# More places for raw weight chunks, W' for two pages in a turn, and casts and exponentials one step later

## The chip, the cores and the metric

One core of a Trainium2 chip. The metric is the device time of one execution in microseconds; of the kernel before, three runs are shown, and one more execution was profiled. The engines run at the same time, each its own instructions in order: TensorE (PE, with weight loads as PEld), VectorE (DVE), ScalarE (ACT), GpSimd (POOL), and SyncE (SP), which here issues nearly all transfers.

## What is computed

An attention with 32 memory slots per head is followed by two layers of a feed-forward network, all in float32. Cut to what matters (4 batches, 8 heads, 576 tokens of 64 values each, 32 slots, 512 model values, 2048 hidden values):

```python
a = softmax(phi, over the 32 slots)            # with + 1e-9 in the divisor
k_m, v_m = einsum(a, k), einsum(a, v)          # per head, over the tokens
attn = softmax(q @ k_m.T / 8, over the slots)
x = (attn @ v_m), heads side by side           # (2304, 512)
h = maximum(x @ w_in, 0); x = h * h @ w_out    # first layer
h = x @ w_in2; out = h * tanh(softplus(h)) @ w_out2   # second layer
```

## The kernel before

**Tiling.** The attention output is never formed. For each batch the kernel makes W' = v_m times w_in (lines 484 to 511), so that h = softmax weights times W'. W' has 8 pages of 256 hidden values; a page serves two steps. Matrix products are made of three matmuls on a value split into a rounded high part and the rest (low part): ScalarE copies the high part, VectorE subtracts to get the low one.

**A tile** (`a_tile`, line 576) is a loop over steps fc, one for each 128 hidden values. A step has 6 matmuls of h = W' times the attention weights (lines 589 to 591), then ScalarE's Relu (597) and square (598), the split into g (602, 605), and, three steps later, 12 matmuls of g with w_out1 into four banks (551 to 553): 18 matmuls. The two halves (288 tokens each) of batches 0 and 1 are done in three groups of 4, 6 and 6 steps, 12 tiles in all (i = 0 to 11, line 729), so that each weight serves four tiles while it is converted. Batches 2 and 3 then take each half in one tile of 16 steps.

**Beside the steps** run: the conversion of the first layer's weights (`Conv`, line 149); the second layer's (`Fold`, line 236), whose results are stored by POOL (312); the memory k_m, v_m of the next batches (`kv_unit`); and the attention weights (`attn_unit`, line 443): score matmuls into a pair of banks, then transpose, maximum, difference (462), exponential (463), sum, product, transpose, and the split into ah and al (478, 479), cut into four parts by `yield`. A `lane` runs one part (or two) in each step. `tick` runs before the Relu of a step, `mid` and `post` after it.

**Conversion.** The weights come as 8-byte numbers, in 32 raw chunks of 512 KB, in the order of `order` (line 615). Count them from 0: chunk 20 is page row i1_10, 21 is i1_11, 22 is o1_10. A step starts one: ScalarE works on the high word (187), VectorE builds the float from bit fields (209, 216), and chunks of w_out are split (182, 224). Pages of w_in are also stored to DRAM (220), to be loaded again for batches 2 and 3 (`load_page`, 723). Nine chunks are loaded ahead; behind the bit fields of chunk n comes the load of chunk n+9 (222). Each load needs a place (`spots`, 623): chunks 0 to 17 have three places of the tag raw and six that later hold w_out1 (tags wo..7, wo..6, wo..5), in turn. From chunk 18 on there are the three raw places alone.

**W'.** `w_part` makes one page: 16 small matmuls into the bank pair "bb" (one buffer, also used by the score matmuls and by the transposes of phi), ScalarE's copy (495) and VectorE's subtraction (496). `w_pair` makes two pages in the two halves of the bank pair, and is used for batch 3 alone.

**Order.** The program is written in the order above, but a scheduler with a timeline of its own places each engine's instructions; earlier written work has the higher priority, and other work is drawn forward when it is ready. `issue_after` (in `behind`, 141) keeps an instruction behind a named one on the same engine. `marks["step"]` is the latest Relu.

Of the kernel before, what the change touches and what calls it, by code (L numbers as in the profile page):

```python
# [38 lines left out]
def body(tc, q, kvm, kvt, phi, w_in1, w_out1, w_in2, w_out2, out):  # L39
# [19 lines left out]
    cm_y, Y = open_pool("y", "right")  # L59
# [78 lines left out]
    marks = {}  # L138

    @contextlib.contextmanager  # L140
    def behind(table, key):

        if key is None:
            yield
        else:
            with tc.issue_after(table[key].ins):
                yield
# [295 lines left out]
    def attn_unit(b, half, nxt=None):  # L443
        n = f"{b}{half}"
        qt = q_t.pop((b, half))
        ps = banks2(f"psc{n}")
        for g in range(4):
            for p in range(2):
                done_pe["psc", b, half] = nc.tensor.matmul(
                    ps[M * g:M * g + M, p, :T], kT[b][D * p:D * p + D, M * g:M * g + M],  # L450
                    qt[g // 2][D * p:D * p + D, g % 2, :], start=True, stop=True)
        if nxt is not None:
            nxt()

        x = Y.tile([P, 2, T], F32, tag="x", name=f"x{n}", bufs=1)
        xv = x.rearrange("p a (c m) -> p (a c) m", m=NB)
        for p in range(2):
            nc.vector.transpose(x[:, p], ps[:, p, :T])
        mx = Y.tile([P, 2 * TB], F32, tag="smx", name=f"smx{n}", bufs=1)
        marks[b, half] = nc.vector.tensor_reduce(out=mx, in_=xv, op=ALU.max, axis=AX.X)  # L460
        yield
        nc.vector.tensor_sub(xv, xv, mx.unsqueeze(2).to_broadcast([P, 2 * TB, NB]))
        nc.scalar.activation(x, x, AF.Exp)
        yield
        sm = Y.tile([P, 2 * TB], F32, tag="ssm", name=f"ssm{n}", bufs=1)
        nc.vector.tensor_reduce(out=sm, in_=xv, op=ALU.add, axis=AX.X)
        nc.vector.tensor_scalar_add(sm, sm, EPS)
        nc.vector.reciprocal(sm, sm)
        nc.vector.tensor_mul(xv, xv, sm.unsqueeze(2).to_broadcast([P, 2 * TB, NB]))
        yield  # L470
        a = Y.tile([P, 2, T], F32, tag="at", name=f"at{n}", bufs=1)
        nc.vector.transpose(a.rearrange("p a t -> p (a t)"), x.rearrange("p a t -> p (a t)"))
        pool = Y if b in (1, 2) else X
        a_t[b, half] = tuple(
            pool.tile([P, 2, T], F32R, tag=f"a{part}", name=f"a{part}{b}{half}", bufs=2)
            for part in "hl")
        hi, lo = a_t[b, half]
        nc.scalar.copy(hi, a)
        marks[b, half] = nc.vector.tensor_sub(lo, a, hi.bitcast(F32))  # L479
        yield  # L480
# [3 lines left out]
    def w_part(b, j, lo, hi):  # L484

        ps = banks2(f"pw{b}{j}{lo}")[:, :, :hi - lo]
        for g in range(4):
            for p in range(2):
                nc.tensor.matmul(  # L489
                    ps[M * g:M * g + M, p], vT[b][D * p:D * p + D, M * g:M * g + M],  # L490
                    wt["i1", j][D * p:D * p + D, g, lo:hi], start=True, stop=True)
        if (b, j) not in wp:
            wp[b, j] = page([P, 2, 2, 256], F32R, f"wp{b}{j}")
        t = wp[b, j]
        nc.scalar.copy(t[:, 0, :, lo:hi], ps)
        nc.vector.tensor_sub(t[:, 1, :, lo:hi], ps, t[:, 0, :, lo:hi].bitcast(F32))  # L496

    def w_pair(b, j):

        ps = banks2(f"pw{b}{j}p")  # L500
        for i in range(2):
            for g in range(4):
                for p in range(2):
                    nc.tensor.matmul(
                        ps[M * g:M * g + M, p, 256 * i:256 * i + 256],
                        vT[b][D * p:D * p + D, M * g:M * g + M],
                        wt["i1", j + i][D * p:D * p + D, g], start=True, stop=True)
        for i in range(2):
            t = wp[b, j + i] = page([P, 2, 2, 256], F32R, f"wp{b}{j + i}")
            nc.scalar.copy(t[:, 0], ps[:, :, 256 * i:256 * i + 256])  # L510
            nc.vector.tensor_sub(t[:, 1], ps[:, :, 256 * i:256 * i + 256], t[:, 0].bitcast(F32))


    y1 = dram.tile([P, 4, NTOK], F32, name="y1")
# [61 lines left out]
    def a_tile(b, half, f0, f1, tick, mid, post, banks=("mm",)):  # L576

        acc = [psum.tile([P, 512], F32, tag=f"acc{d}", name=f"a{b}{half}{f0}{d}") for d in range(4)]
        done = evac_y1(b, half, f0 == 0, f1 == NF)
        hi, lo = a_t[b, half]  # L580
        for fc in range(f0, f1):
            n = f"{b}{half}_{fc}"
            w = wp[b, fc // 2]
            fs = slice((fc % 2) * P, (fc % 2) * P + P)
            ph = hbank(banks[fc % len(banks)], f"h{n}")[:, :T]
            key = ahead.get((b, half, fc))
            for hg in range(2):
                with behind(done_pe, key if hg == 0 else None):
                    nc.tensor.matmul(ph, w[:, 0, hg, fs], hi[:, hg], start=(hg == 0), stop=False)  # L589
                nc.tensor.matmul(ph, w[:, 0, hg, fs], lo[:, hg], start=False, stop=False)  # L590
                nc.tensor.matmul(ph, w[:, 1, hg, fs], hi[:, hg], start=False, stop=(hg == 1))  # L591
            tick(fc)
            flush()
            s = X.tile([P, T], F32, tag="s", name=f"s{n}", bufs=3)
            g = X.tile([P, 2, T], F32R, tag="g", name=f"g{n}", bufs=4)
            sh, sl = g[:, 0], g[:, 1]
            marks["step"] = nc.scalar.activation(s, ph, AF.Relu)  # L597
            nc.scalar.activation(s, s, AF.Square)

            def rest(s=s, sh=sh, sl=sl):  # L600
                if b < 3:
                    nc.scalar.copy(sh, s)  # L602
                else:
                    nc.vector.tensor_copy(sh, s)
                marks["lo"] = nc.vector.tensor_sub(sl, s, sh.bitcast(F32))  # L605

            later.append(rest)
            mid(fc)
            pend.append((mm2_step, (acc, fc, fc == f0, fc == f1 - 1, sh, sl, done)))
            run_pend(LAG)  # L610
            post(fc)


    bounds = [sum(GROUPS[:i]) for i in range(len(GROUPS) + 1)]
    order = []
    for f0, f1 in zip(bounds, bounds[1:]):
        order += [("i1", f0), ("i1", f0 + 1)]
        for f in range(f0, f1, 2):
            order.append(("o1", f))
            if f + 2 < f1:  # L620
                order += [("i1", f + 2), ("i1", f + 3)]
            order.append(("o1", f + 1))
    spots = [(Y, "raw", 3)] * 3 + [
        (wo, f"wo{part}{j}", 1) for j in (7, 6, 5) for part in "hl"]

    c1 = Conv(order, lambda i: spots[i % 9 if i < 18 else i % 3],
              lambda key, u: key != "i1" or u < 8 or (1, u // 2 - 4) in wp)
    c1.limit = 2 * GROUPS[0]
    c1.load(1)
# [37 lines left out]
    def lazy(f):  # L667
        yield from f()
# [19 lines left out]
    def attn_later(b, half):  # L688
        def nxt():
            if b < 2:  # L690
                if (b, half) == (0, 1):
                    load_q(1, 1)
                elif (b, half) == (1, 0):
                    load_q(2, 0)
                return
            nb, nh = (b, 1) if half == 0 else (b + 1, 0)
            if nb < B:
                load_q(nb, nh)
        return [[lazy(lambda: attn_unit(b, half, nxt)), 4]]


    subs = [(f0, f1, b, half) for f0, f1 in zip(bounds, bounds[1:])
# [20 lines left out]
    def load_page(j):  # L723

        wt["i1", j] = Y.tile([P, 4, 256], F32, tag="i1", name=f"win1r_{j}", bufs=4)
        nc.sync.dma_start(wt["i1", j], w1[j])

    lanes, n_steps = [], 1
    for i, (f0, f1, b, half) in enumerate(subs):
        final = i == len(subs) - 1  # L730
# [37 lines left out]
            run_step(lanes, n_steps)  # L768

        def post(fc):  # L770
            if fc % 2 == half == 0 and fc + 2 < f1 and i != 2:
                c1.need("i1", fc + 3)
                w_part(b, fc // 2 + 1, 0, 256)
            if i == 1 and fc + 1 == f1:
                w_part(1, fc // 2, 0, 256)
            if i % 4 == 0:
                if fc >= f0 + 2:
                    c1.need("o1", fc - 2)
                if fc + 1 == f1:
                    c1.need("o1", fc)  # L780
            if half == 1 and fc + 2 == f1 and not final:

                if b == 0:
                    w_part(1, f0 // 2, 0, 256)
                else:
                    c1.need("i1", f1 + 1)
                    w_part(0, f1 // 2, 0, 256)
            if final and fc < f1 - 1:
                w_part(2, fc - f0, 0, 256)
                if fc < f1 - 2:  # L790
                    load_page(fc - f0 + 2)

        if i == 0:
            w_part(0, 0, P, 2 * P)
# [17 lines left out]
            run_step(lane)  # L812

    def post(fc):
        if fc in (0, 2, 4):
            load_page(5 + fc // 2)
        if fc in (3, 5, 7):
            w_part(b, 5 + fc // 2 - 1, 0, 256)
        if fc == NF - 1:
            for j in range(4):  # L820
                load_page(j)
# [13 lines left out]
    drain(*lanes)  # L835


    while fold.busy():
        fold.tick()
    close(cm_psum2)  # L840
# [125 lines left out]
    now = 0  # L966
# [216 lines left out]
```

## Time and profile before

| | us |
|---|---|
| median of 3 runs | 766.96 (763.28 to 769.29) |
| the profiled execution | 767.97 |
| its span, first to last instruction | 766.1 |
| TensorE busy | 731.6 |
| VectorE busy | 530.1 |
| ScalarE busy | 424.8 |
| mean granted TensorE clock | 0.981 |

The busy time is a share of a span that has stages of different kinds: conversion and attention of batches 0 and 1 until about 200 us, batch 2 from 222.9, batch 3 from 318.2, and the second layer from 389.9 us on. PEclk is the clock that TensorE was granted, as a share of 2.4 GHz. A wait is put down to the instruction that released it. "Idle before" counts the time in which that engine did nothing before the instruction. Matmuls overlap, so the time from one start to the next tells more than the duration.

### The profile page before, as it was taken

To read this page: it belongs to the slowest core of one execution; us is meant where nothing else is said; L and a number is where in the kernel's file an instruction comes from. 1 tells how busy PE (TensorE), PEld (TensorE's weight loads), DVE (VectorE), ACT (ScalarE), POOL (GpSimd) and SP (SyncE) were. 2 spreads that over 40 slices of the span, in tenths; PEclk is the share of its full clock that TensorE was granted. 3 is DMA by queue.
4 is the path that set the end of the run, shared out by engine and by line. 5 is a ranking of instruction groups with operands and counts; after the bars stand their busy time and mean duration, and the time that the engine had idled before them with its cause. 6 is when DMAs were issued, how large, how long until landed. Compare 5 with 4: busy or idle time off the path is not lost.

```text
span 766.1 us, 15325 instructions
## 1 busy us (share of the span) xinstructions
PE 731.6 (95%) x5480; PEld 691.6 (90%) x5480; DVE 530.1 (69%) x1072; ACT 424.8 (55%) x960; POOL 130.9 (17%) x176
## 2 busy tenths in 40 slices
PE   5699799999999999999999999999999999999997
PEld 4487798998887889999999899989999989999997
DVE  3989835527587679787897856894756794556583
ACT  3677845756566678767665435652434652334552
POOL 0000000000121223323322401140411050111040
PEclk8699999999999999999999999999999999999999
DMA  8993505406898878787969989888977888787882
GB/s 330 404 409 108 174 20 195 136 1 214 309 324 280 305 242 314 275 313 238 364 211 324 343 250 364 250 256 276 339 244 264 252 256 290 235 267 240 263 271 73
DMA packets 87900, 195.80 MB, mean 256 GB/s; under 512 B 9872, under 2 KB 21136, under 8 KB 87824
## 3 DMA queue, kind: packets, MB, share of 16 engines
q1 hardware_dynamic: 78864, 165.45, 64.7%
q0 software_dynamic: 8960, 29.37, 9.7%
q8 instruction: 44, 0.72, 0.4%
q14 instruction: 32, 0.26, 0.1%
HBM read 151.78 MB, written 42.99 MB: 254 GB/s over the span
## 4 chain that ended last, share of the span: by engine, by line
PE 78%; DVE 7%; DMA 5%; ACT 5%; issue 3%; SPq 0%; POOL 0%; DVEq 0%; POOLq 0%; ACTq 0%
PE hb L995 7%; PE a L551 7%; PE hb L996 7%; PE hb L997 7%; PE a L553 7%; PE a L552 7%; PE h L589 4%; PE h L590 3%; PE h L591 3%; DMA raw_i<-in_moe_w_in_dram 2%; PE pw L489 1%; DVE opl L1040 1%; DMA yr<-y 1%; DMA raw_o<-in_moe_w_out_dram 1%; PE pk L407 1%
## 5 line engine op out<-in xcount | busy, mean ns | idle before, releaser
L551 PE MATMUL a<-g,o1h 128*128 128x288 f32 x512 | 150.2, 302 | 3.3 <-ACT g L602 3.3
L552 PE MATMUL a<-g,o1l 128*128 128x288 f32 x512 | 148.4, 298 | 0.0
L553 PE MATMUL a<-g,o1h 128*128 128x288 f32 x512 | 131.1, 298 | 0.4 <-DVE g L605 0.4
L1040 DVE TENSOR_TENSOR opl<-a,oph 128x384 fp32r<-128x384 f32 x144 | 92.9, 664 | 44.9 <-ACT oph L1039 44.3
L995 PE MATMUL hb<-ych,u 128*128 128x384 f32 x336 | 113.3, 337 | 2.7 <-DVE hs L1005 1.4
L996 PE MATMUL hb<-ycl,u 128*128 128x384 f32 x336 | 113.0, 336 | 0.0
L997 PE MATMUL hb<-ych,u 128*128 128x384 f32 x336 | 110.2, 336 | 0.0
L1039 ACT CAST oph<-a 128x384 fp32r<-128x384 f32 x144 | 73.9, 513 | 61.2 <-PE b22acc L1060 8.0
L551 PEld LDWEIGHTS a<-g,o1h 128*128 128x128 f32 x512 | 96.9, 190 | 10.5 <-ACT g L602 6.0
L552 PEld LDWEIGHTS a<-g,o1l 128*128 128x128 f32 x512 | 97.2, 190 | 0.0
L553 PEld LDWEIGHTS a<-g,o1h 128*128 128x128 f32 x512 | 89.9, 190 | 5.2 <-issue 1.8
L597 ACT ACTIVATE s<-h 128x288 f32<-128x288 f32 x128 | 52.7, 412 | 70.1 <-PE h L591 62.6
L1001 ACT ACTIVATE a<-hs 128x384 f32<-128x384 f32 x72 | 37.6, 525 | 96.4 <-DVE hs L1005 96.4
L589 PE MATMUL h<-ah,wp 128*128 128x288 f32 x256 | 79.7, 313 | 7.5 <-ACT s L597 3.8
L605 DVE TENSOR_TENSOR g<-s,g 128x288 fp32r<-128x288 f32 x128 | 57.7, 452 | 33.3 <-ACT g L602 31.9
L312 POOL DMA_DIRECT2D wf_i<-st x56 | 30.4, 545 | 281.9 <-DVE st L311 266.7
L591 PE MATMUL h<-ah,wp 128*128 128x288 f32 x256 | 76.7, 300 | 0.7 <-DVE wp L496 0.7
L590 PE MATMUL h<-al,wp 128*128 128x288 f32 x256 | 76.7, 300 | 0.3 <-DVE al L479 0.3
L1005 DVE TENSOR_TENSOR hs<-hu,hb 128x384 f32<-128x384 f32 x72 | 39.6, 552 | 42.1 <-PE hb L997 41.7
L995 PEld LDWEIGHTS hb<-ych,u 128*128 128x128 f32 x336 | 63.0, 188 | 3.7 <-DMA u<-wf_i 1.9
L589 PEld LDWEIGHTS h<-ah,wp 128*128 128x128 f32 x256 | 48.6, 191 | 17.6 <-ACT s L597 6.7
L996 PEld LDWEIGHTS hb<-ycl,u 128*128 128x128 f32 x336 | 63.0, 188 | 0.0
(255 smaller groups left out, 1571.9 us busy)
## 6 DMA issues: line engine op xcount, KB each, us to landing
u<-wf_i SPq DMA_DIRECT2D x168, 256.0 KB, 3.8
u<-wf_o SPq DMA_DIRECT2D x168, 256.0 KB, 3.4
raw_i<-in_moe_w_in_dram SPq DMA_DIRECT2D x32, 512.0 KB, 5.6
raw_o<-in_moe_w_out_dram SPq DMA_DIRECT2D x32, 512.0 KB, 7.3
wf_i<-st POOLq DMA_DIRECT2D x56, 256.0 KB, 4.9
wf_o<-st POOLq DMA_DIRECT2D x56, 256.0 KB, 4.6
win1r<-w_i SPq DMA_DIRECT2D x17, 512.0 KB, 5.4
kv<-in_kvm_dram SPq DMA_DIRECT2D x5, 1024.0 KB, 9.3
```

Source lines behind the costliest of these rows:

```text
L551: nc.tensor.matmul(o, wh[:, c, cs], sh, start=first, stop=False)
L552: nc.tensor.matmul(o, wl[:, c, cs], sh, start=False, stop=False)
L553: nc.tensor.matmul(o, wh[:, c, cs], sl, start=False, stop=last)
L589: nc.tensor.matmul(ph, w[:, 0, hg, fs], hi[:, hg], start=(hg == 0), stop=False)
L590: nc.tensor.matmul(ph, w[:, 0, hg, fs], lo[:, hg], start=False, stop=False)
L591: nc.tensor.matmul(ph, w[:, 1, hg, fs], hi[:, hg], start=False, stop=(hg == 1))
L605: marks["lo"] = nc.vector.tensor_sub(sl, s, sh.bitcast(F32))
L995: nc.tensor.matmul(ps, wh, yh[:, d], start=(j < 4 and d == 0), stop=False, **kw)
L996: nc.tensor.matmul(ps, wh, yl[:, d], start=False, stop=False, **kw)
L997: nc.tensor.matmul(ps, wl, yh[:, d], start=False, stop=end, **kw)
L1039: marks["hi"] = nc.scalar.copy(hi, x)
L1040: marks["lo"] = sub(lo, x, hi.bitcast(F32))
```

## The change

- `place` gives chunks 21, 22, 23, 24, 28 and 29 places of the tags wo..7 and wo..6 in place of raw ones.
- For batches 2 and 3 the exponential comes one `yield` behind the difference; the unit then has five parts.
- `w_pair` puts its copies and subtractions into a list, and `w_out` issues them in the next step behind Relu and square, ScalarE's copies ordered behind that Relu; `now=True` issues them at once.
- Single pages become pairs: at the first step of the tiles i = 6 and i = 10 (batch 1, first half; at once), in the last tile, i = 11 (pages 0 to 3 of batch 2), and in the first tile of batch 2 (pages 4 to 7). The second load of page 5 goes.

```diff
--- before.py
+++ after.py
@@ -460,6 +460,8 @@
         marks[b, half] = nc.vector.tensor_reduce(out=mx, in_=xv, op=ALU.max, axis=AX.X)
         yield
         nc.vector.tensor_sub(xv, xv, mx.unsqueeze(2).to_broadcast([P, 2 * TB, NB]))
+        if b > 1:
+            yield
         nc.scalar.activation(x, x, AF.Exp)
         yield
         sm = Y.tile([P, 2 * TB], F32, tag="ssm", name=f"ssm{n}", bufs=1)
@@ -495,7 +497,15 @@
         nc.scalar.copy(t[:, 0, :, lo:hi], ps)
         nc.vector.tensor_sub(t[:, 1, :, lo:hi], ps, t[:, 0, :, lo:hi].bitcast(F32))
 
-    def w_pair(b, j):
+    wait_w = []
+
+    def w_out(late=False):
+        for f in wait_w:
+            with behind(marks, "step" if late else None):
+                f()
+        wait_w.clear()
+
+    def w_pair(b, j, now=False):
 
         ps = banks2(f"pw{b}{j}p")
         for i in range(2):
@@ -505,10 +515,17 @@
                         ps[M * g:M * g + M, p, 256 * i:256 * i + 256],
                         vT[b][D * p:D * p + D, M * g:M * g + M],
                         wt["i1", j + i][D * p:D * p + D, g], start=True, stop=True)
-        for i in range(2):
+
+        def take(i):
             t = wp[b, j + i] = page([P, 2, 2, 256], F32R, f"wp{b}{j + i}")
             nc.scalar.copy(t[:, 0], ps[:, :, 256 * i:256 * i + 256])
             nc.vector.tensor_sub(t[:, 1], ps[:, :, 256 * i:256 * i + 256], t[:, 0].bitcast(F32))
+
+        for i in range(2):
+            if now:
+                take(i)
+            else:
+                wait_w.append(lambda i=i: take(i))
 
 
     y1 = dram.tile([P, 4, NTOK], F32, name="y1")
@@ -596,6 +613,7 @@
             sh, sl = g[:, 0], g[:, 1]
             marks["step"] = nc.scalar.activation(s, ph, AF.Relu)
             nc.scalar.activation(s, s, AF.Square)
+            w_out(True)
 
             def rest(s=s, sh=sh, sl=sl):
                 if b < 3:
@@ -623,7 +641,14 @@
     spots = [(Y, "raw", 3)] * 3 + [
         (wo, f"wo{part}{j}", 1) for j in (7, 6, 5) for part in "hl"]
 
-    c1 = Conv(order, lambda i: spots[i % 9 if i < 18 else i % 3],
+    deep = dict(zip((21, 22, 23, 24, 28, 29), (3, 4, 5, 6, 3, 4)))
+
+    def place(i):
+        if i in deep:
+            return spots[deep[i]]
+        return spots[i % 9] if i < 18 else (Y, "raw", 3)
+
+    c1 = Conv(order, place,
               lambda key, u: key != "i1" or u < 8 or (1, u // 2 - 4) in wp)
     c1.limit = 2 * GROUPS[0]
     c1.load(1)
@@ -696,7 +721,7 @@
             nb, nh = (b, 1) if half == 0 else (b + 1, 0)
             if nb < B:
                 load_q(nb, nh)
-        return [[lazy(lambda: attn_unit(b, half, nxt)), 4]]
+        return [[lazy(lambda: attn_unit(b, half, nxt)), 5 if b > 1 else 4]]
 
 
     subs = [(f0, f1, b, half) for f0, f1 in zip(bounds, bounds[1:])
@@ -768,7 +793,10 @@
             run_step(lanes, n_steps)
 
         def post(fc):
-            if fc % 2 == half == 0 and fc + 2 < f1 and i != 2:
+            if half == 0 and b == 1 and f1 - f0 == 6:
+                if fc == f0:
+                    w_pair(b, fc // 2 + 1, True)
+            elif fc % 2 == half == 0 and fc + 2 < f1 and i != 2:
                 c1.need("i1", fc + 3)
                 w_part(b, fc // 2 + 1, 0, 256)
             if i == 1 and fc + 1 == f1:
@@ -785,10 +813,10 @@
                 else:
                     c1.need("i1", f1 + 1)
                     w_part(0, f1 // 2, 0, 256)
-            if final and fc < f1 - 1:
-                w_part(2, fc - f0, 0, 256)
-                if fc < f1 - 2:
-                    load_page(fc - f0 + 2)
+            if final and fc - f0 in (1, 3):
+                w_pair(2, fc - f0 - 1)
+            if final and fc < f1 - 2:
+                load_page(fc - f0 + 2)
 
         if i == 0:
             w_part(0, 0, P, 2 * P)
@@ -812,10 +840,10 @@
             run_step(lane)
 
     def post(fc):
-        if fc in (0, 2, 4):
-            load_page(5 + fc // 2)
-        if fc in (3, 5, 7):
-            w_part(b, 5 + fc // 2 - 1, 0, 256)
+        if fc in (0, 2):
+            load_page(6 + fc // 2)
+        if fc in (2, 5):
+            w_pair(b, 4 + 2 * (fc == 5))
         if fc == NF - 1:
             for j in range(4):
                 load_page(j)
@@ -835,6 +863,7 @@
     drain(*lanes)
 
 
+    w_out()
     while fold.busy():
         fold.tick()
     close(cm_psum2)
```

## Rows read from the trace of the kernel before

**Rows 1.** The page, busy time: us, share of the span, instructions.

```profile
PE 731.6 (95%) x5480; PEld 691.6 (90%) x5480; DVE 530.1 (69%) x1072; ACT 424.8 (55%) x960; POOL 130.9 (17%) x176
```

**Rows 2.** Table by stage: us; busy time (instructions) per engine; PEclk; DMA share, GB/s.

```profile
60.00:86.00 26.00, 24.38 (x226) 20.41 (x225) 24.96 (x55) 22.11 (x54) 0.00 (x0) 1.00 0.25 85
86.00:102.00 16.00, 12.59 (x83) 11.03 (x82) 9.11 (x20) 8.34 (x21) 0.00 (x0) 0.79 0.50 166
102.00:200.00 98.00, 98.00 (x816) 90.69 (x814) 49.78 (x108) 59.50 (x140) 3.39 (x6) 1.00 0.42 137
320.00:388.00 68.00, 68.00 (x515) 68.00 (x514) 54.17 (x136) 45.57 (x113) 17.55 (x33) 1.00 0.78 278
```

**Rows 3.** Waits of TensorE, 60:102 and 200:320: us in total, times, longest.

```profile
PE h L589 <- ACT s L597: 3.4, 2, 3.0
PE a L551 <- ACT g L602: 2.9, 4, 1.0
```

**Rows 4.** ScalarE in order of time, 20:105: start, us, instruction, [idle before <-releaser].

```profile
86.90 0.69 ACT L187 ACTIVATE raw_i<-raw_i 128x512 f32<-128x512 f32 x1 [0.50 <-DMA raw_i<-in_moe_w_in_dram]
91.41 0.67 ACT L187 ACTIVATE raw_o<-raw_o 128x512 f32<-128x512 f32 x1 [2.72 <-DMA raw_o<-in_moe_w_out_dram]
```

**Rows 5.** SP in order of time, 60:96: start, us, the issue.

```profile
83.31 0.33 SPq L166 DMA_DIRECT2D raw_i<-in_moe_w_in_dram  x1
84.79 0.33 SPq L166 DMA_DIRECT2D raw_o<-in_moe_w_out_dram  x1
```

**Rows 6.** TensorE in order of time, 58:105.

```profile
88.75 0.40 PE L589 MATMUL h<-ah,wp 128*128 128x288 f32 x1 [0.46 <-ACT s L597]
92.77 0.61 PE L589 MATMUL h<-ah,wp 128*128 128x288 f32 x1 [2.95 <-ACT s L597]
```

**Rows 7.** VectorE in order of time, 20:130.

```profile
61.74 1.29 DVE L216 SCALAR_TENSOR_TENSOR win<-raw_i,win 128x512 int32<-128x512 int32 x2
91.42 0.43 DVE L209 TENSOR_SCALAR ct_o<-raw_o 128x512 int32<-128x512 int32 x1 [2.52 <-DMA raw_o<-in_moe_w_out_dram]
94.02 0.45 DVE L605 TENSOR_TENSOR g<-s,g 128x288 fp32r<-128x288 f32 x1
```

**Rows 8.** Table by stage again, shorter stretches, 70 to 99 us.

```profile
70.00:80.00 10.00, 8.45 (x79) 6.59 (x79) 9.61 (x22) 8.14 (x20) 0.00 (x0) 1.00 0.04 17
92.00:96.00 4.00, 3.23 (x20) 2.96 (x25) 3.69 (x9) 3.76 (x12) 0.00 (x0) 0.51 0.60 206
96.00:99.00 3.00, 3.00 (x25) 2.19 (x25) 0.86 (x2) 0.93 (x2) 0.00 (x0) 0.51 0.25 100
```

**Rows 9.** TensorE in order of time, 173.7:308.2; and the line of pairs, L504.

```profile
173.78 0.29 PE L591 MATMUL h<-ah,wp 128*128 128x288 f32 x1
174.00 0.64 PE L489 MATMUL pw<-win,vT 64*32 64x256 f32 x8
174.57 0.40 PE L589 MATMUL h<-ah,wp 128*128 128x288 f32 x1
306.47 1.09 PE L504 MATMUL pw34p<-win1r,vT 64*32 64x256 f32 x32
L504 PE MATMUL pw30p<-win1r,vT x32: 376/388/400, 268.3 to 274.0; 64*32 64x256 f32 x32
```

**Rows 10.** ScalarE (200:300) and TensorE (234:240) in order of time.

```profile
233.69 0.42 ACT L310 CAST st<-raw_i 128x256 fp32r<-128x256 f32 x1 [2.61 <-DMA wf_i<-st]
238.12 0.68 ACT L463 ACTIVATE x<-x 128x576 f32<-128x576 f32 x1 [1.66 <-DVE x L462]
234.97 0.40 PE L551 MATMUL a<-g,o1h 128*128 128x288 f32 x1 [0.88 <-ACT g L602]
```

**Rows 11.** VectorE (200:300) and TensorE (222.8:227) in order of time.

```profile
222.73 0.75 DVE L479 TENSOR_TENSOR al<-at,ah 128x576 fp32r<-128x576 f32 x1
225.29 0.30 PE L590 MATMUL h<-al,wp 128*128 128x288 f32 x1
226.62 0.40 PE L589 MATMUL h<-ah,wp 128*128 128x288 f32 x1 [0.37 <-ACT s L597]
```

## Prediction

> **What bounds the kernel now.** I read the page's busy times first: TensorE is busy 731.6 of 766.1 us [rows 1], so what can be won is its idle time, its time at the lower clock, and matmul work that can be shortened. The table by stage says where that lies [rows 2]. From 102 to 200 us TensorE is busy 98.00 of 98 us, from 320 to 388 us all 68 (515 matmuls, so 0.132 us each, and 2.38 for a step of 18): nothing to win there. From 86 to 102 us it has 12.59 of 16 us at a mean granted clock of 0.79: the worst stage. The waits by pairs name the losses [rows 3]: until 102 us, 3.4 us for the Relu; from 200 to 320 us, 2.9 us in four waits for ScalarE's cast of g.
>
> The first loss is no ScalarE work. ScalarE stands 0.50 us and then 2.72 us in front of the exponent-field operation of L187 because raw chunks 21 and 22 have not landed, and VectorE stands 2.52 us for the second too [rows 4, 7]. The next Relu is queued behind it, and TensorE waits 2.95 us for that [rows 6]. SP issued these loads only at 83.31 and 84.79 us [rows 5]; by the code they wait until VectorE has read a chunk in one of the three raw places. After the wait the first matmul of h takes 0.61 us, where it took 0.40 after the wait before it [rows 6], and the clock is 0.51 from 92 to 99 us, the 1.2 GHz level; from 70 to 80 us it was 1.00 [rows 8].
>
> **The change, part by part.** *Raw places.* The load of chunk n+9 is put down behind the bit fields of chunk n, so 21 and 22 come behind 12 and 13; by the old rule they also waited for a raw place, by the new one they take the wo places that 12 and 13 leave. Chunks 11 and 12 leave theirs at 61.74 + 1.29 = 63.03 us [rows 7]. So load 21 goes out some 20 us earlier, 22 right behind it, and both land in time even at the 91.41 - 84.79 = 6.62 us that load 22 took [rows 4, 5]; from 70 to 80 us the DMA engines are at 0.04 [rows 8], so nothing is pushed aside. SP issues no more; these loads pass the store of a finished chunk pair, which waits for VectorE and not for them. Chunks 28 and 29 wait for 21 and 22 to be read, long before. The order of conversion stays: its starts hang on the steps.
> What goes: 2.95 + 0.46 = 3.4 us of waiting [rows 6], and 6.2 us at half clock (92.77 to 99), worth at most 3.1: together 6.5. What is late next is VectorE. From 91.42 to the end of its g subtraction at 94.02 + 0.45 it works through 3.05 us [rows 7]. Moved up by its own 2.52 us wait, that subtraction ends near 91.95. TensorE, at h again at 88.29 instead of 88.75, wants it after twelve h matmuls and three products, 15 x 0.132 = 2.0 us, near 90.3. A new wait of 1.7, so the term is **4.8 us** (bounds: 2, if VectorE takes still more; 6.5).
>
> *Pairs.* Six pairs take the place of twelve single pages: one in each of two tiles of batch 1's first half, two in the last tile of batch 1, two in the first of batch 2. Matmuls, casts and subtractions stay the same in number. A page holds TensorE for 0.64 us, a pair for 1.09 [rows 9] (the first and last of a page's 16 matmuls are among the 8 recorded): 2 x 0.64 - 1.09 = 0.19, and one time fewer the next matmul takes 0.40 instead of 0.29: 0.3 for each pair, 1.8 for six. But an existing pair was scattered, from 268.3 to 274.0 us [rows 9], and each further piece costs some 0.3 again. Taken: **1.0** (bounds -1 and 1.8). Page 5, loaded twice before, is loaded once: one transfer fewer, on no path.
>
> *Casts a step later.* No instruction is added; ScalarE's copy is ordered behind the next Relu, so it cannot hold that Relu back while TensorE is still before the page's matmuls. One wait for a Relu in this region is 0.37 us [rows 11]. The price: the bank pair stays full a step longer, and the score matmuls and phi transposes are next in line for it. Their steps move too, and their results are wanted many steps later, except at one place (below).
>
> *Exponential a step later.* ScalarE waits 1.66 us for VectorE's difference at 238.12 [rows 10], and TensorE behind it for the cast of g, the longest of the four waits, 1.0 us [rows 3]. That goes. A second, 0.88 us at 234.97, comes from a staging buffer whose store has not landed (ScalarE 2.61 us at 233.69) [rows 10]; the change leaves it alone. Of the other two, 2.9 - 1.0 - 0.88 = 1.0, I take half. Taken: 1.0 + 0.4 + 0.5 = **1.9** (bounds 1.0 and 3.3, all five waits).
>
> *What that costs.* For batch 2's first half the attention result is used right at the start of the next tile. Its low part is done at 222.73 + 0.75 = 223.48, and its first reader runs at 225.29 [rows 11]: 1.81 us of slack. A step later (2.38), and behind one W' subtraction more (0.6, an estimate from the 1.29 us that two operations of 512 columns take [rows 7]), it comes 2.38 + 0.6 - 1.81 = 1.2 us late. VectorE loses one of five pages in this stretch, so I take **-1.0** (bounds 0 and -4).
>
> Sum: 4.8 + 1.0 + 1.9 - 1.0 = **6.7 us**. The profiled execution took 767.97 us (span 766.1), 1.0 above the median shown, 766.96. So 761.3 for the execution, 760.3 against the median. A measurement of this kernel can tell about 1% from no change, 7.7 us: below 759.3 is faster, above 774.6 slower.
>
> **Rivals.** *B, more falls away.* The waits of rows 3 go, VectorE keeps up, pairs stay whole: 6.5 + 3.3 + 1.8 = 11.6: 755.4. For it: casts spread over more steps. Against: VectorE has 24.96 of 26 us from 60 to 86 us [rows 2].
> *C, VectorE takes the gap.* The loads land, but VectorE, nearly full since 60 us, is what TensorE then waits for, and the region from 200 us trades one wait for another. The first term at about 3 and the others at nothing: 764.
> *D, the clock stays low all the same.* The 2.95 us wait becomes two or three short ones and the clock falls on these: 2.8 us of the first term stay, 763. The Trainium skill, "TensorE: Matmul & The Clock Gate", section "A second HAM failure mode: psum-queue depth-cycling", says that frequent short idles between groups of matmuls make the clock swing; by that rule it would go this way. Against it stands the stretch from 70 to 80 us, 1.55 us idle and the clock at 1.00 [rows 8].
> *E, slower.* The place is the handover into batch 2. The low part hangs on a chain of five stages, each behind other work of VectorE. If the extra stage costs two steps, TensorE waits 2 x 2.38 + 0.6 - 1.81 = 3.6 us, more than the 2.95 after which the clock fell, and pays the half clock again: 3.1. With pairs scattered (-1) and 3 from the first term that is 4.7 slower: 771.7. It decides once the low part lands some 3 us after TensorE's backlog ends. For: the chain has only 1.81 us to spare. Against: one page's work has left this stretch.
> *F, it doesn't act.* The order of issue keeps the loads behind the store that SP waits on; they land just in time or not, under 2 us won: 766.
>
> **Chances and numbers.** Forecast 0.45 (its own range 757.5 to 763), B 0.20, C 0.19, D 0.04, E 0.08, F 0.04. Below 759.3 lie B and nearly half of the forecast's chance: faster 0.40. Above 774.6 lies a part of E: slower 0.05. The rest, 0.55, is within 1%. The range 754.5 to 766.0 leaves out E, half of F and an end of B, under 0.2.
>
> **What would show it.** Chunks 21 and 22 issued before 80 us, and no wait of L187 for a DMA after 86 us; the clock at 1.00 from 92 to 99 us; the dense stage behind it begun some 5 us earlier; the 32 matmuls of a pair in one piece; no ScalarE wait for the difference. Wrong would be: loads still behind a wait on SP, VectorE named for TensorE's waits near 90 us, or TensorE idle for over 1.5 us where batch 2 begins.

## The result, and the profile after

The changed kernel takes 759.13 us (median of 6 runs, 758.01 to 761.76); the kernel before took 767.10 in the runs beside it (6 runs, 763.28 to 769.29). The ratio is 0.9908, with an interval of 0.9882 to 0.9933. The profiled execution took 760.09 us, against 767.97 before. Its page: the span, and the busy times of the engines.

```profile
span 758.3 us, 15324 instructions
...
PE 728.6 (96%) x5480; PEld 691.1 (91%) x5480; DVE 529.9 (70%) x1072; ACT 425.1 (56%) x960; POOL 131.1 (17%) x176
```

The span is 7.8 us shorter, with the same instructions on the engines [rows 1]. Of these 7.8 us, 3.0 are TensorE's busy time (731.6 to 728.6) and 4.8 its idle time. I found them in three places. The table by stage, in the stretches of [rows 2, 8], shows the first. Its columns: stretch and length, busy time (and instructions) of PE, PEld, DVE, ACT and POOL, granted clock, DMA share, GB/s.

```profile
86.00:102.00 16.00, 16.00 (x121) 14.27 (x121) 9.12 (x21) 10.16 (x26) 0.00 (x0) 1.00 0.50 171
92.00:96.00 4.00, 4.00 (x32) 4.00 (x31) 1.59 (x5) 1.45 (x5) 0.00 (x0) 1.00 0.69 278
96.00:99.00 3.00, 3.00 (x25) 3.00 (x24) 1.00 (x3) 1.48 (x4) 0.00 (x0) 1.00 0.00 0
```

TensorE is busy for all 16 us where it had 12.59, at a clock of 1.00 where it had 0.51 from 92 to 99. The cause stands in SP's list (start, duration, issue): the loads of chunks 21 and 22, which SP issued at 83.31 and 84.79 before [rows 5].

```profile
63.47 0.38 SPq L166 DMA_DIRECT2D raw_i<-in_moe_w_in_dram  x1
63.94 1.28 SPq L166 DMA_DIRECT2D raw_o<-in_moe_w_out_dram  x1
```

ScalarE's next operations on them, where it had stood 0.50 and 2.72 us [rows 4], have no idle time in front (a bracket behind a row gives it where there is some):

```profile
84.44 0.69 ACT L187 ACTIVATE raw_i<-raw_i 128x512 f32<-128x512 f32 x1
86.48 0.70 ACT L187 ACTIVATE raw_o<-raw_o 128x512 f32<-128x512 f32 x1
```

The second place is TensorE's waits from 110 to 320 us (total, times, longest). They add up to 1.4 us. Before, the same view has the 2.9 us of [rows 3] and 0.4 each for a Relu and for the scores, 3.7 together.

```profile
PE h L606 <- ACT s L614: 1.2, 1, 1.2
PE a L568 <- ACT g L620: 0.2, 1, 0.2
```

The third is W' itself. TensorE in order of time (start, duration, instruction): three pieces of one page, then a whole pair. A row with x4 is four matmuls in one piece.

```profile
86.24 0.29 PE L569 MATMUL a<-g,o1l 128*128 128x288 f32 x1
86.46 0.62 PE L491 MATMUL pw<-win,vT 64*32 64x256 f32 x4
87.02 0.40 PE L606 MATMUL h<-ah,wp 128*128 128x288 f32 x1
87.25 0.30 PE L607 MATMUL h<-al,wp 128*128 128x288 f32 x1
...
88.53 0.64 PE L491 MATMUL pw<-win,vT 64*32 64x256 f32 x10
...
89.87 0.29 PE L608 MATMUL h<-ah,wp 128*128 128x288 f32 x1
90.09 0.62 PE L491 MATMUL pw<-win,vT 64*32 64x256 f32 x2
90.64 0.40 PE L606 MATMUL h<-ah,wp 128*128 128x288 f32 x1
90.88 0.30 PE L607 MATMUL h<-al,wp 128*128 128x288 f32 x1
...
200.98 0.29 PE L608 MATMUL h<-ah,wp 128*128 128x288 f32 x1
201.26 1.10 PE L514 MATMUL pw20p<-win1r,vT 64*32 64x256 f32 x32
202.29 0.40 PE L606 MATMUL h<-ah,wp 128*128 128x288 f32 x1
202.53 0.30 PE L607 MATMUL h<-al,wp 128*128 128x288 f32 x1
```

Read the starts. Large matmuls start every 0.132 us. After 89.87 the next would have started at 90.00; it starts at 90.64, and the one behind it 0.24 later. A piece is a run of small matmuls with no large one between them. So a piece of two small matmuls takes 0.64 + 0.11 = 0.75 us of TensorE. The piece of four takes as much (0.65 + 0.10), the pair of 32 takes 1.18 + 0.11 = 1.29, and other whole pairs 1.21. **Up to 16 matmuls the price is one per piece, hardly one per matmul.** Larger pieces cost half as much again, but hardly by their number either: read in the same way, one of 22 (at 222.27 us) takes 1.18 and one of 24 (at 113.83 us) 1.19. The Trainium skill, "TensorEngine Tiling (Array Packing)", section "Key Properties", says that a change of tiling mode drains TensorE; these rows agree, with 0.75 us for a turn to the small shape and back.

**Where the 7.8 us come from.** I followed the start of each step's h matmuls through both traces. Steps are counted over all tiles, 0 to 127. Steps 10 to 15 start within 0.02 us of those before, step 20 0.36 later (TensorE waits 0.80 us for VectorE's bit fields at 79.28, where it waited 0.47), step 22 5.61 earlier (96.30 for 101.91): the stage of the loads. Step 34 is 5.98 ahead, step 80, half way through batch 2, 7.96, and steps 96 to 127 8.68. The part behind step 127 is 0.87 us longer (378.41 for 377.54); it lies between 376.4 and 380.2 in the traces of the experiments (e9 and e10 left out), so it is not laid to the change.

### The profile page after: what moved, and what is told of

It reads as the page before. It is cut to its first block, busy times and chain, and to the rows that moved or that the text cites. A ratio compares the mean times of both kernels' runs of the same rounds, so it can differ in the third digit from the quotient of the medians.

```text
span 758.3 us, 15324 instructions
## 1 busy us (share of the span) xinstructions
PE 728.6 (96%) x5480; PEld 691.1 (91%) x5480; DVE 529.9 (70%) x1072; ACT 425.1 (56%) x960; POOL 131.1 (17%) x176
## 5 line engine op out<-in xcount | busy, mean ns | idle before, releaser
L1024 PEld LDWEIGHTS hb<-ych,u 128*128 128x128 f32 x336 | 63.6, 189 | 3.8 <-DVE hs L1034 2.1
L1026 PEld LDWEIGHTS hb<-ych,u 128*128 128x128 f32 x336 | 63.4, 189 | 0.0
```

What stands on the lines that cost most here:

```text
L1024: nc.tensor.matmul(ps, wh, yh[:, d], start=(j < 4 and d == 0), stop=False, **kw)
L1026: nc.tensor.matmul(ps, wl, yh[:, d], start=False, stop=end, **kw)
```

## The experiments

A ratio is to the kernel before in runs beside it on the same chip, with a 95% interval. There were three such groups: e1, e2, e5 and e6; e3, e4, e7 and e8; e9 to e12. The median of before in them was 765.84, 766.92 and 767.99 us.

**Is it the places?** Places alone, and the change without them:

```diff
 # e1_places_alone: before.py
-    c1 = Conv(order, lambda i: spots[i % 9 if i < 18 else i % 3],
+    deep = dict(zip((21, 22, 23, 24, 28, 29), (3, 4, 5, 6, 3, 4)))
+    def place(i): ...
+    c1 = Conv(order, place,
 # e2_no_places: after.py
-    deep = dict(zip((21, 22, 23, 24, 28, 29), (3, 4, 5, 6, 3, 4)))
+    deep = {}
```

> The kernel before with the new places of the raw chunks alone. Theory (the late loads of chunks 21 and 22 make the stage from 86 to 102 us): 5.0 to 6.0 us faster than before, the stage after it begun at 96 to 97 us instead of 101.9, no wait of L187 for a DMA near 87 us, clock 1.00 from 92 to 99 us, and the region from 200 us on unchanged but for its start. Rival (the gain needs the pairs or the exponential's step): under 2 us. Rival (VectorE takes the gap): about 3 us, with VectorE as the releaser of TensorE's waits near 90 us.

> The changed kernel with the old raw places. Theory: the waits of 0.5 and 2.7 us near 87 and 91 us and the half clock after them come back as they were; the rest of the change is worth 2 to 3 us, so 764 to 765. Rival (places do it all and the rest trades waits): 767, as before. Rival (parts are not additive, the second region gains only when it starts earlier): slower than before by 1 us or more.

Measured: places alone 764.38 us, ratio 0.9988 (0.9969 to 1.0007); the change without them 763.17, 0.9969 (0.9943 to 0.9994). By the medians places alone are worth 1.5 us, though their interval holds 1, and the rest alone 2.7. Together they were 8.0, so the parts don't seem to add up; but the changed kernel had no runs in this group, so a part of the gap can lie between the groups.

The trace of places alone (ahead by some 0.28 us at steps 10 to 15, which I take off) does show the stage as forecast: at step 22 it is 5.62 us ahead of the profiled execution of before, as the changed kernel is. At step 34 it is 4.11 ahead, at step 127 3.72. TensorE's list shows where 1.5 us go again. Here are a page in two pieces, and below a whole one.

```profile
104.06 0.64 PE L489 MATMUL pw<-win,vT 64*32 64x256 f32 x8
104.62 0.40 PE L589 MATMUL h<-ah,wp 128*128 128x288 f32 x1
...
113.54 0.64 PE L489 MATMUL pw<-win,vT 64*32 64x256 f32 x8
...
223.01 0.29 PE L591 MATMUL h<-ah,wp 128*128 128x288 f32 x1
223.24 0.66 PE L489 MATMUL pw<-win1r,vT 64*32 64x256 f32 x16
223.83 0.40 PE L551 MATMUL a<-g,o1h 128*128 128x288 f32 x1
224.07 0.29 PE L552 MATMUL a<-g,o1l 128*128 128x288 f32 x1
```

A whole page takes (223.83 - 223.14) + 0.11 = 0.80 us, hardly more than a piece of two or four. Before makes two pages between steps 18 and 22, each in one piece:

```profile
85.04 0.66 PE L489 MATMUL pw<-win,vT 64*32 64x256 f32 x16
...
95.94 1.11 PE L489 MATMUL pw<-win,vT 64*32 64x256 f32 x16
```

With the loads early, the first comes in three pieces ahead of step 22 (at 86.17, 88.24 and 89.80), and the second behind it, in the two shown: 2 x 0.76 = 1.5 us after the stage that were in it before. From 84 us until batch 3 is made I count, by this reading of the starts, 29 pieces for before, which take 23.8 us (in its second profile, below, where none of them is lengthened by the low clock), 32 and 26.0 us with places alone, and 25 and 23.0 in the changed kernel. So early loads on single pages cost three pieces, 2.2 us. With places alone TensorE's waits of batch 2 stay too (110 to 320 us):

```profile
PE a L551 <- ACT g L602: 3.3, 4, 1.3
PE h L589 <- ACT s L597: 0.4, 1, 0.4
PE psc L449 <- ACT kT L423: 0.4, 1, 0.4
```

The change without places keeps the late loads (84.15 us for chunk 22), but its stall is small. TensorE's longest wait there, and the table by stage:

```profile
91.41 0.40 PE L606 MATMUL h<-ah,wp 128*128 128x288 f32 x1 [2.30 <-ACT s L614]
```

```profile
86.00:92.00 6.00, 3.29 (x23) 2.82 (x22) 4.01 (x10) 3.75 (x10) 0.00 (x0) 1.00 0.88 287
92.00:96.00 4.00, 4.00 (x42) 3.42 (x41) 2.77 (x7) 3.27 (x9) 0.00 (x0) 1.00 0.62 206
```

No half clock, and with a second wait of 0.41 no more than 2.7 us of waiting to win there.

**How many places?** On the kernel before:

```diff
 # e5_two_places: before.py, place() as in the change, and
+    deep = {21: 3, 22: 4}
 # e6_one_place: the same, and
+    deep = {21: 3}
```

> The kernel before with new places for chunks 21 and 22 alone. Theory: the same as with all six to within 0.5 us (5 to 6 us faster than before), since chunks 23 and later are started only from about 105 us on. Rival (loads 23 and 24 matter too, or the load of 25 is held up): 2 us or more behind the run with all six.

> The kernel before with a new place for chunk 21 alone; chunk 22 then takes the first raw place that comes free, about 83.3 us instead of 84.8, and lands near 88 to 90 us. Theory: ScalarE still waits 0 to 2 us for chunk 22 and TensorE somewhat less; if TensorE's idle time stays below 2 us the clock stays at 1.00, and 3 to 5 us of the 5 to 6 are kept. Rival (the clock falls on a short wait as well): TensorE waits about 1 us, the clock is at half level for some 6 us after it, and only 1.5 to 2.5 us are kept.

Measured: 764.99 us, ratio 0.9987 (0.9966 to 1.0009), and 764.25, 0.9988 (0.9967 to 1.0008): by the time neither can be told from six places, nor from before. The trace says more. With one place, SP's list, ScalarE's first operation on chunk 22, and the table by stage:

```profile
64.21 0.38 SPq L166 DMA_DIRECT2D raw_i<-in_moe_w_in_dram  x1
...
84.08 0.33 SPq L166 DMA_DIRECT2D raw_o<-in_moe_w_out_dram  x1
```

```profile
87.75 0.69 ACT L187 ACTIVATE raw_o<-raw_o 128x512 f32<-128x512 f32 x1
```

```profile
86.00:102.00 16.00, 16.00 (x122) 14.27 (x121) 9.53 (x21) 11.15 (x28) 0.00 (x0) 1.00 0.47 155
```

Chunk 21 goes out at 64.21 us, 22 still at 84.08, into the raw place that 21 would have taken. It comes in time all the same: with no other load just ahead of it, ScalarE starts on it 3.67 us later, without idle time in front. So on the kernel before, one place of the six is enough to take the stall away, which I had not seen; with the pairs it was not tried.

**How large is the stall of before?** One more profiled execution of it, unchanged:

> The kernel before, unchanged, for a second look at its trace. Theory (how long chunk 22 is waited for, and with it the half clock, differs from execution to execution): a wait of ScalarE between 0.5 and 3 us near 90 us, and the stage behind it begun somewhere from 97 to 102 us, with the loads issued at the same places in the order. Rival (the stall is the same each time): 2.7 us again and the stage begun at 101.5 to 102.

It took 765.47 us. ScalarE, TensorE, and the table by stage:

```profile
86.33 0.69 ACT L187 ACTIVATE raw_i<-raw_i 128x512 f32<-128x512 f32 x1 [0.43 <-DMA raw_i<-in_moe_w_in_dram]
...
90.47 0.67 ACT L187 ACTIVATE raw_o<-raw_o 128x512 f32<-128x512 f32 x1 [2.35 <-DMA raw_o<-in_moe_w_out_dram]
```

```profile
91.82 0.61 PE L589 MATMUL h<-ah,wp 128*128 128x288 f32 x1 [2.58 <-ACT s L597]
```

```profile
86.00:102.00 16.00, 13.01 (x97) 11.97 (x96) 8.71 (x20) 9.22 (x23) 0.00 (x0) 0.89 0.50 160
92.00:96.00 4.00, 4.00 (x32) 3.43 (x33) 2.95 (x7) 3.18 (x10) 0.00 (x0) 0.67 0.65 220
96.00:99.00 3.00, 3.00 (x25) 3.00 (x25) 1.83 (x4) 1.43 (x4) 0.00 (x0) 1.00 0.02 7
```

The wait is 0.37 us shorter than in [rows 6], and the lower level ends before 96 us, not at 99 [rows 8]. Less a head start of 0.52 us, step 22 comes 1.87 us earlier than in the first profile, step 127 2.42. So **the stall has no one size**. Against this profile the places win 5.62 - 1.87 = 3.8 us at step 22 and 3.72 - 2.42 = 1.3 at step 127, which is what the medians show. Over 35 runs before ranged from 761.59 to 770.31; 15 of them lie above 766.20. Of the 36 runs with six, two or one places, 3 do. So early loads seem to take away the bad executions more than to speed up the good ones. What the stall is in before's best executions no trace shows.

**Pairs or delays?** The two delays undone one by one and together, one left off where batch 2 begins, and the later exponential with places but with single pages:

```diff
 # e3_exp_at_once: after.py
-        if b > 1:
-            yield
-        return [[lazy(lambda: attn_unit(b, half, nxt)), 5 if b > 1 else 4]]
+        return [[lazy(lambda: attn_unit(b, half, nxt)), 4]]
 # e4_cast_at_once: after.py
-            if now:
+            if True:
 # e11_places_and_pairs: after.py with both of these
 # e8_exp_not_first: after.py, that unit again with four parts, and
-        if b > 1:
+        if b > 1 and n != "20":
             yield
 # e7_single_pages: before.py, place() and the five parts as in the change, and
+        if b > 1:
+            yield
```

> The changed kernel with the softmax exponential again in the step of its difference (four parts). Theory: ScalarE's wait of 1 to 2 us for the difference comes back in one of batch 2's units and TensorE waits about 1 us for it; but the attention result of batch 2's first half comes a step earlier: 0 to 1.5 us slower than the changed kernel. Rival (the step more costs at the handover into batch 2 what it gives later): 0.5 us faster or equal.

> The changed kernel with the copies and subtractions of every pair issued at once. Theory (a cast in front of the next Relu holds it while TensorE is still before the pair's matmuls): ScalarE waits 1 to 4 us for TensorE's pair matmuls in several places, TensorE loses 0.5 to 1.5 us: 0.5 to 1.5 us slower than the changed kernel. Rival (the scheduler puts the cast behind the Relu in any case): equal within 0.3 us.

> The changed kernel without both of its one-step delays: exponentials and casts at once, places and pairs as changed. Theory (places and pairs make the whole gain): within 1 us of the changed kernel, 759 to 761. Rival (each delay can stand in for the other, and one of them is needed): 1.5 us or more slower than the changed kernel.

> The changed kernel with the exponential a step later in all units but that of batch 2's first half, whose result is wanted at once. Theory (the step more costs TensorE about 1 us at the handover into batch 2): 0.5 to 1 us faster than the changed kernel. Rival (TensorE has enough product matmuls in hand there): equal within 0.3 us, or slower if the unit's exponential again waits for its difference.

> The kernel before with the new raw places and the exponential a step later, but W' in single pages cast at once, and batch 3's pairs as before. Theory (six pairs save 0.3 us each, less where one is scattered, and casts a step later take a wait away): 1 to 2.5 us slower than the changed kernel. Rival (pairs and late casts give nothing): equal within 0.3 us.

| | us | ratio | interval |
|---|---|---|---|
| e3, exponential at once | 760.44 | 0.9908 | 0.9893 to 0.9923 |
| e4, casts at once | 759.88 | 0.9899 | 0.9883 to 0.9915 |
| e11, both at once | 759.39 | 0.9902 | 0.9875 to 0.9929 |
| e8, exponential not late for batch 2's first half | 759.42 | 0.9895 | 0.9877 to 0.9912 |
| e7, places, late exponential, single pages | 765.14 | 0.9982 | 0.9966 to 0.9998 |

**Places and pairs without any delay (e11) make the whole gain.** Neither delay is worth anything that these runs can tell, and the late exponential costs nothing at the handover. TensorE's waits from 110 to 320 us in e11:

```profile
PE h L604 <- ACT s L612: 1.2, 2, 0.7
PE a L566 <- ACT g L618: 0.7, 1, 0.7
```

and in e7 (the row left out is 0.4 us):

```profile
PE a L553 <- ACT g L604: 3.7, 4, 1.7
PE h L591 <- ACT s L599: 0.4, 1, 0.4
...
```

With pairs and no delay they are 1.9 us, with the delay of the exponential and no pairs 4.5. The waits for the cast of g go with the pairs.

**What are the pairs worth once the places are there?** e4 and e7 answer that, for they ran side by side and differ in the pairs alone (with the steps at which they are made, and the second load of page 5). The medians differ by 5.3 us, and the slowest run of e4 (761.23) is faster than the fastest of e7 (763.69). The traces show where it goes. At step 127 e4 is 4.7 us further ahead than e7, each counted from its head start at step 15. Its pieces, 25 for 32, take 3.0 us less, and its waits from 110 to 320 us are 2.6 us for 4.5. Without the places the same pairs, with the delays, brought 2.7 (e2).

**What is one piece worth by itself?** Each page or pair held together by a block that the scheduler does not take apart:

```diff
 # e9_whole_pages: e1 / e10_whole_pairs: after.py
-        (matmul loops of w_part and w_pair)
+        with tc.tile_critical():
+            (the same loops)
```

> The kernel before with all six raw places, single pages, and the matmuls of a page (or of batch 3's pairs) kept together in one piece; nothing else of the change. W' then stands in 29 pieces on TensorE, where the places alone had 40, the kernel before 37 and the changed one 33. Theory (what the pairs gave is fewer pieces: each turn to the small matmuls and back costs 0.4 to 0.6 us): 4 to 6 us faster than the places alone, so 759 to 761. Rival (the pairs gave fewer casts in front of a Relu, or a better time for them): within 1.5 us of the places alone, 763 to 765.

> The changed kernel with the matmuls of each page or pair kept in one piece: 23 pieces in place of 33. Theory (pieces cost 0.4 to 0.6 us each): 3 to 5 us faster than the changed kernel, 754.5 to 756.5. Rival (pieces fill gaps in which TensorE would wait anyway): within 1 us of the changed kernel, or slower where a whole pair of 1.1 us holds back h.

Measured: 858.26 us, ratio 1.1190 (1.1158 to 1.1222), and 850.02, 1.1077 (1.1042 to 1.1111). TensorE's list in e9 says why:

```profile
35.63 0.93 PE L490 MATMUL pw<-win,vT 64*32 64x128 f32 x16 [16.17 <-DMA kv11v<-in_kvm_dram]
...
145.28 1.11 PE L490 MATMUL pw<-win,vT 64*32 64x256 f32 x16 [6.66 <-DMA raw_o<-in_moe_w_out_dram]
```

The first is batch 0's first page, and kv11v belongs to batch 1; the second waits for a chunk of w_out, which W' does not use. The block waits for transfers that are none of its business. The pieces do come down (29 and 23 over the whole program, from 40 and 33), but holding them together costs 856.5 - 762.5 = 94 us by the spans of e9 and e1. So this says nothing on the price of a piece; that is read from the starts alone.

## Why the prediction came out, and which steps did not

The time was forecast at 760.3 us against the median and 761.3 for the execution; measured were 759.13 and 760.09. The mechanism of the first stage was right. Part of the rest came out right for other reasons than mine, and that the sum fits the medians is in part luck. By the medians places alone bring 1.5 us where I had 4.8, and pairs on top of them 5.3 where I had 1.9 for all the rest: the sums are alike, the shares are not.

- **Raw places, 4.8.** In this pair of executions the term measures 4.1 us at step 34 (places alone), and 4.9 without the piece that its second page gets more than before. Issue before 80 us, no wait of L187, clock at 1.00: all as said. The new VectorE wait of 1.7 us did not come near 90 us; the wait at 79 us grew by 0.3. With both chunks long landed, the conversion lies spread over the steps before, not packed behind 91 us. Two more pieces of the first page took its place, 1.5 us. What I did wrong is to take the stall of one execution for that of the kernel: against the second profile, and by the medians, places alone bring 1.3 to 1.5.
- **Pairs, 1.0.** The row of [rows 9] at 174.00 was not a page with eight matmuls unrecorded, but one of two pieces of eight: before has another of eight at 158.95, and no W' matmul is missing from its trace. Since a piece of eight costs nearly what a whole page does, "0.3 for each pair" is nearly right all the same (two pages 2 x 0.79, a pair 1.21: 0.37). "Each further piece costs some 0.3 again" is the step that failed: it costs 0.75, and I let scattered pairs eat half of the gain, while four of the six new ones came whole. Leaving out the page that the places scatter, before's pieces take 23.8 - 0.8 = 23.0 us and the changed kernel's 23.0 - 2.25 = 20.8: 2.2, above my bound of 1.8, and 6 x 0.37. Against places alone it is 26.0 - 23.0 = 3.0.
- **Casts and exponential a step later, 1.9.** The waits did shrink, by 3.7 - 1.4 = 2.3 us, of which 1.6 are left as a remainder in the end (below): the size was about right and the cause wrong. e11 has them small without any delay, e7 has them large with one. ScalarE's wait for the difference did not go either, it fell from 1.66 to 1.0, and it is 0.9 in e11 without the delay; in the changed kernel, from 195 to 315 us (total, times, longest):

```profile
ACT x L465 <- DVE x L462: 1.0, 1, 1.0
```

- **Handover, -1.0.** Not seen. From step 64 to step 65 TensorE has no wait in the changed kernel (the longest, 1.20 us, comes 12 us later, at 231.76), and e8 (0.9895) stands within the intervals of e4 and e11.

So at step 127 the traces show 4.9 + 2.2 = 7.1 us for places and pairs, and 8.7 in all: the 1.6 between is a remainder, left for the waits. 0.9 go again behind that step: 7.8, where I had 4.8 + 1.0 + 1.9 - 1.0 = 6.7. The two terms that I had most wrong, pairs and handover, were both too low.

**The rivals.** B's 755.4 is not reached: 1.2 us of waiting stay in batch 2, two of the new pairs lie in two pieces, and an old one is still scattered. C (VectorE) and D (the clock falls on short waits) fall by the table: 16.00 of 16 us at 1.00. E (slower at the handover) falls by the missing wait there and by e8. F falls by SP's list.

**What stays open.** Why single pages scatter more once the loads come early, and why ScalarE's casts of g are in time with pairs, is known from comparing kernels only; the scheduler's choice was not tried by itself. By the medians places and pairs bring some 4 us more together than apart (8.0 against 1.5 + 2.7), or 2.6 if the pairs' worth on top of the places is taken from e4 and e7 (5.3 against 2.7). The pieces account for 2.6: places on single pages cost 26.0 - 23.8 = 2.2 us of them, places on top of pairs save 0.4 (23.5 in e2, 23.0 after). Whether anything is left beyond that these runs don't settle.

## What to carry to other kernels

Before a stall is priced from one profile, profile the same kernel twice: a wait for a transfer that is only just late differs from run to run, and the time at the lower clock behind it with it. Where small matmuls of another shape lie between large ones, count the pieces, not the matmuls, and see whether an edit elsewhere changes that count. And two edits that each bring little alone can bring much together: test both before dropping either.

## What the runs showed of the hardware

- A turn of TensorE to the small 64 x 32 shape and back takes 0.75 us with 2 matmuls, 0.80 with 16, 1.18 with 22 and 1.2 to 1.3 with 32.
- TensorE's clock stayed at 1.00 after an idle time of 2.30 us (e2). After 2.58 us it was at a mean of 0.67 from 92 to 96 us and at 1.00 behind that; after 2.95 us it stood at 0.51, the 1.2 GHz level, until 99 [rows 6, 8]. These are three executions, and no rule is drawn from them.
- Chunk 22's load, issued 1.5 us behind that of chunk 21, took 6.6 us until ScalarE, waiting, could start on it, 6.2 in the second profile (84.29 to 90.47). Issued with no load near ahead of it (e6) it took at most 3.67, and ScalarE did not wait.
